# Fused attention and two MoE blocks on one core: q rounded on ScalarE one step sooner, and the first chunk's set-up put in another order

## The chip, the cores and the metric

The kernel runs on 1 core of a Trainium2 chip. The time is device microseconds of one execution of the whole kernel; the figure given for a kernel is the median of its runs, and lower is better.

## The reference

Talking-heads attention over 4 batches of 12 heads (448 positions, head size 64), and behind it two feed-forward blocks over 1792 tokens of width 768, all in float32.

```
scores = scale * q @ k.T                      # per batch and head
scores = einsum('bhij,hg->bgij', scores, w_pre)
attn   = softmax(scores over j)               # eps 1e-9 in the sum
attn   = einsum('bhij,hg->bgij', attn, w_post)
x      = attn @ v
a, b   = x @ w1, x @ w2
x      = ((a * b) @ w3) @ w_out               # first block
h      = relu(x @ w_in)
out    = (h * h) @ w_out2                     # second block
```

## The kernel before

**Rounding in two parts.** TensorE multiplies rounded operands here. So q and k are each split into a rounded "high" part and a "low" rest. For q, `high_q` (L254) writes `qh` from the raw `qraw`, and `low_q` (L262) writes `ql = qraw - qh` on GpSimd. For k, the raw keys are loaded twice, in both halves of the 128 partitions; `high_k` (L231) rounds all of them into `kt`, and `low_k` (L239) replaces the lower half by the rest, in two pieces of 64x448, one for each of the two heads of the tile. `scores` (L271) then needs two matmuls per head, one with `qh` and one with `ql`.

**Chunks, blocks, steps.** The query rows of a batch are cut into 4 chunks (110, 110, 110, 118 rows), 16 chunks in all. A chunk's scores for 12 heads are evacuated to the tile `s` (`evac`, L287). `regroup` (L296) moves them by DMA, SBUF to SBUF, into blocks `r` of up to 120 partitions (10 rows by 12 heads), 11 or 12 blocks per chunk, 180 in all. Per block there is a head mix on TensorE (`premix`, L305, tile `sp`), a row maximum on VectorE (`nm`), the exponential with its sum on ScalarE (`expo`, L317), a split of the probabilities into two f16 parts, and the second mix (`tmix`, L367). `pv` (L416) multiplies by v, twice per chunk. A step of the main loop handles two blocks; step d mixes blocks 2d and 2d+1, and moves blocks 2d+4 and 2d+5.

**What sets the order.** The order is written out by hand, and each engine works its queue strictly in that order. `attention_plan` (L445) puts a chunk's `scores`, and ahead of them `load_q`, `high_q` and `low_q`, on steps; `attention_step` (L492) issues them. In a step SyncE (SP) first issues the regroups, then the loads of q, k and v. `ORDER` (L475) gives each engine's order within a step: VectorE's list ends with `high_q`, `high_k`; `low_q` follows one step behind `high_q`. There are 2 buffers for `qraw`, 2 for `sp`, 6 for `r`.

**The start (L922 to L956).** SP issues q and k loads of chunk 0, then `setup_load` (the tiles `eye`, `w2a`, `w2b`), then the last two k loads, which wait for buffers. Heads 0 to 11 of chunk 0 follow in pairs, with `setup_pre` (it makes the mixing matrix `kpre`) in between. In the first chunk ScalarE does `high_k` and `high_q`, VectorE does both pieces of `low_k`, and evacuations alternate. `setup_post` (the factors of the second mix, with one small matmul `pc`, L207) comes after step -1, that is directly ahead of the first `premix`. `load_v` of batch 0 is issued in step 0. For chunk 1 `load_q` and `high_q` lie in the steps from -5 on, and the scores in the steps from -2 on.

After the attention the two feed-forward blocks run on TensorE, with `mm3` (L53) at its core; nothing of that is changed.

Of the kernel before, what the change touches and what calls it, by code (L numbers as in the profile page):

```python
# [36 lines left out]
def fused_kernel(ctx, tc, q, k, v, w_pre, w_post, w1, w2, w3t, wo, win, wo2, eye, out):  # L37
# [124 lines left out]
    class Attention:  # L162
# [17 lines left out]


        def setup_load(self):
            nc.sync.dma_start(self.eye, eye)
            for t, w in ((self.w2a, w_pre), (self.w2b, w_post)):
                nc.sync.dma_start(t, w)

        def setup_pre(self):
            e, w = self.eye, self.w2a
# [7 lines left out]
        def setup_post(self):  # L196
            kw, kab, ones = (self.kc.tile([120, S], F, tag="p", name=x, bufs=5) for x in ("kw", "kab", "ones"))
            kw, kab = (x[:, :120].rearrange("p (g i) -> p g i", i=10) for x in (kw, kab))
            ones = ones[:, :128]
            nc.vector.memset(ones, 1.0)  # L200
            nc.vector.tensor_tensor(
                kw, self.eye.unsqueeze(1).to_broadcast([120, 12, 10]),
                self.w2b.unsqueeze(2).to_broadcast([120, 12, 10]), ALU.mult,
            )
            nc.vector.tensor_scalar(kab.bitcast(I32), kw.bitcast(I32), 0x7FFFFFFF, None, ALU.bitwise_and)
            pc = self.ps.tile([128, 120], F, tag="sp", name="pc", bufs=2)
            nc.tensor.matmul(pc, ones, kab.rearrange("p g i -> p (g i)"), start=True, stop=True)  # L207
            m, u = self.wm, self.wu
            nc.vector.tensor_reduce(m, pc, AX.X, ALU.max)
            nc.vector.tensor_scalar(m, m, 2.0**-98, None, ALU.max)  # L210
            nc.vector.tensor_scalar(m.bitcast(I32), m.bitcast(I32), 0x7F800000, None, ALU.bitwise_and)
            nc.vector.reciprocal(u, m)
            nc.vector.tensor_scalar(self.iv, m, 2.0**-27, None, ALU.mult)
            nc.vector.memset(self.ivm, 0.0)
            for z in range(2):
                half = slice(64 * z, 64 * z + 64)
                nc.vector.tensor_copy(self.ivm[half, z : z + 1], self.iv[half])
            nc.vector.tensor_scalar(kw, kw, u[:120], 2.0**13, ALU.mult, ALU.mult)
            kh, kl = self.khl
            nc.vector.tensor_copy(kh, kw)  # L220
            nc.vector.tensor_tensor(kl, kw, kh, ALU.subtract)
# [17 lines left out]
        def low_k(self, b, r):  # L239
            raw, t = self.kraw.pop((b, r)), self.kt[b, r]  # L240
            for e in range(2):
                eng = nc.gpsimd if b else nc.vector
                eng.tensor_tensor(t[64:128, e], raw[64:128, e], f32(t[64:128, e]), ALU.subtract)  # L243
            self.done.add(("k", b, r))

# [8 lines left out]
        def high_q(self, n, g4):  # L254
            th = self.ka.tile([128, 4 * IC], R, tag="qh", name=f"qh{n}_{g4}", bufs=3)
            th = self.qh[n, g4] = th[:, : 4 * CHUNKS[n % 4][1]]
            if n:
                nc.vector.tensor_copy(th, self.qraw[n, g4])
            else:
                nc.scalar.activation(th, self.qraw[n, g4], AF.Copy)  # L260

        def low_q(self, n, g4):  # L262
            tl = self.ka.tile([128, 4 * IC], R, tag="ql", name=f"ql{n}_{g4}", bufs=3)
# [181 lines left out]
    def attention_plan():  # L445
# [2 lines left out]
        def add(step, kind, *a):  # L448
            ev.setdefault(step, {}).setdefault(kind, []).append(a)

        lo = {n: (first[n - 1] - 1 - RG) // 2 + 1 for n in range(1, 16)}
        for n in range(16):
            b = n // 4
            if n:
                hi = (first[n] - RG) // 2
                for h in range(NH):
                    t = lo[n] + h * (hi - lo[n]) // NH
                    add(t, "scores", n, h)
                    if h % 4 == 0:
                        add(t - 3, "load_q", n, h // 4)  # L460
                        add(t - 2, "high_q", n, h // 4)
            for y in range(2):
                add((first[n + 1] + 5 + (5 if n < 15 else 0) * y) // 2, "pv", n, y)
        for b in range(1, B):
# [2 lines left out]
                add(t - 1, "load_k", b, r)  # L467
                add(t, "high_k", b, r)
        for b in range(B):
            add((first[4 * b] - 6) // 2 if b else 0, "load_v", b)  # L470
        return ev

    ORDER = (  # L475
        ("premix", "scores", "tmix", "pv"),
        ("expo", "evac", "p_hi", "p2_act", "pv_out"),
        ("rowmax", "p_lo", "norm_recip", "p2_dve", "high_q", "high_k"),
        ("norm_add", "low_q", "low_k"),
    )  # L480
    NEEDS = {
# [433 lines left out]
    with tc.manual_schedule(), ExitStack() as base:  # L915
# [6 lines left out]
        A.load_q(0, 0)  # L922
        A.load_k(0, 0)
        A.load_k(0, 1)
        A.load_q(0, 1, nc.scalar)
        for r in (2, 3):
            A.load_k(0, r)
        A.setup_load()
        for r in (4, 5):
            A.load_k(0, r)  # L930
        for x in range(NH // 2 + 1):
            if x == 0:
                A.split_q(0, 0)
                A.load_q(0, 2)
            if x == 2:
                A.split_q(0, 1)
            if x == 3:
                A.setup_pre()
            if x == 4:
                A.split_q(0, 2)  # L940
            if x < NH // 2:
                A.high_k(0, x)
                A.low_k(0, x)
                for h in (2 * x, 2 * x + 1):
                    A.scores(0, h)
            if x:
                for h in (2 * x - 2, 2 * x - 1):
                    A.evac(0, h)
        step = iter(range(-5, (first[16] + 5) // 2 + 2))
        closed = (first[15] - RG) // 2  # L950
        M = Moe(pre)
        tail = M.tail_plan()
        for d in step:
            attention_step(A, d, ev)
            if d == -1:
                A.setup_post()  # L956
            if d == closed:
                sa.close()
                M.place(pool(sa, "wp"))
# [72 lines left out]
```

## Time and profile before

| | us |
|---|---|
| median of 3 runs | 1325.92 |
| lowest and highest of them | 1325.01, 1327.96 |
| the profiled execution | 1324.3 |
| its span, first to last instruction | 1322.5 |

| engine | busy us | share of the span |
|---|---|---|
| PE (TensorE matmul) | 1284.4 | 97% |
| DVE (VectorE) | 865.6 | 65% |
| ACT (ScalarE) | 696.8 | 53% |
| POOL (GpSimd) | 470.1 | 36% |

The page of the profile gives busy shares of each engine over the span; the views of the trace give single instructions with their start in microseconds from the first instruction, how long the engine was idle before them, and what ended that wait. PE's busy time is modelled from pipelined matmuls, so a matmul whose successor was late can look longer than it worked.

### The profile page before, as it was taken

The numbers are of one execution on the slowest core, as the hardware profiler recorded it, in microseconds if no ns is written. First come the engines' busy times: TensorE is split into PE (matmuls) and PEld (weight loads), VectorE is DVE, ScalarE is ACT, GpSimd is POOL, SyncE is SP. The second block draws the span as 40 slices with busy tenths as digits, with TensorE's granted clock in tenths as the row PEclk, the third lists the DMA queues.
The fourth block names the chain that finished last, engine by engine and source line by source line (L and its number), as shares of the span: only waits on it lengthen the run. The fifth ranks groups of instructions, "written<-read, shape, count | busy, mean of one in ns | idle before, by whom it ended". The sixth has DMA issues, their size and how long they took to land.

```text
span 1322.5 us, 23360 instructions
## 1 busy us (share of the span) xinstructions
PE 1284.4 (97%) x8516; PEld 1111.8 (84%) x8516; DVE 865.6 (65%) x1585; ACT 696.8 (53%) x1542; POOL 470.1 (36%) x522
## 2 busy tenths in 40 slices
PE   5999999999998999999999999999999999999998
PEld 3677776776775788899999999999999999999998
DVE  4899899899879876643127833769565337735742
ACT  4887878787877654443224533534344225534530
POOL 1265255245324512002222322336767322322331
PEclk7999999999999999999999999999999999999999
DMA  5666466566566667655123432463221233433441
GB/s 177 187 178 197 125 197 199 140 173 199 162 159 186 194 196 220 218 164 155 62 81 103 136 116 80 121 220 98 93 62 58 66 92 108 157 94 82 128 147 52
DMA packets 99399, 184.51 MB, mean 140 GB/s; under 512 B 20949, under 2 KB 68053, under 8 KB 98773
## 3 DMA queue, kind: packets, MB, share of 16 engines
q1 hardware_dynamic: 87333, 173.00, 43.9%
q10 hardware_dynamic: 11952, 10.03, 2.3%
q8 instruction: 67, 1.10, 0.3%
q14 instruction: 47, 0.39, 0.1%
HBM read 124.01 MB, written 20.45 MB: 109 GB/s over the span
## 4 chain that ended last, share of the span: by engine, by line
PE 76%; DVE 9%; issue 6%; DMA 3%; POOL 3%; ACT 2%; SPq 0%; POOLq 0%; ACTq 0%; DVEq 0%
PE l L57 39%; PE y L57 9%; PE p L57 5%; PE sp L308 5%; PE tp L373 4%; PE sc L282 3%; DVE pl L364 3%; PE pv L425 3%; DVE nm L314 2%; DMA kraw<-k 1%; DVE p L387 1%; DMA qraw<-q 1%; DMA r<-s 1%; POOL wl L142 1%; POOL ql L265 1%
## 5 line engine op out<-in xcount | busy, mean ns | idle before, releaser
L142 POOL TENSOR_TENSOR wl<-f,wh 128x384 fp32r<-128x384 f32 (+1 forms) x144 | 166.8, 1159 | 468.6 <-ACT wh L114 448.4
L98 DVE TENSOR_SCALAR f<-y 128x384 int32<-128x384 int32 (+1 forms) x176 | 133.4, 758 | 88.2 <-ACT y L86 87.6
L308 PE MATMUL sp<-r,kpre 120*120 120x448 f32 x360 | 158.7, 562 | 10.2 <-ACT p L322 6.8
L322 ACT ACTIVATE p<-sp,nm 120x448 f32<-120x448 f32 x180 | 113.5, 641 | 72.5 <-DVE nm L314 72.2
L364 DVE SCALAR_TENSOR_TENSOR pl<-p,sm,ph 120x448 f16<-120x448 f32 (+3 forms) x270 | 142.0, 579 | 0.3 <-POOL ph L350 0.3
L57 PE MATMUL l<-bhh,wh 128*128 128x448 f32 x384 | 139.3, 363 | 0.0
L57 PE MATMUL l<-blh,wh 128*128 128x448 f32 x384 | 138.8, 362 | 0.0
L57 PE MATMUL l<-bhh,wl 128*128 128x448 f32 x384 | 138.7, 361 | 0.0
L114 ACT ACTIVATE wh<-f 128x384 fp32r<-128x384 f32 (+1 forms) x160 | 89.9, 562 | 74.2 <-DVE f L100 66.7
L100 DVE SCALAR_TENSOR_TENSOR f<-raw,f 128x384 int32<-128x384 int32 (+1 forms) x176 | 124.5, 708 | 6.1
L314 DVE TENSOR_REDUCE nm<-sp 120x1 f32<-120x448 f32 x180 | 106.7, 617 | 24.8 <-PE sp L308 20.9
L373 PEld LDWEIGHTS <-ph 120*128 120x128 f16 x1260 | 93.0, 98 | 30.2 <-issue 22.6
L348 ACT ACTIVATE ph<-p,sm 120x448 f16<-120x448 f32 (+1 forms) x180 | 107.5, 660 | 19.9 <-DVE sm L342 15.7
L282 PE MATMUL sc<-kt,qh 128*110 128x448 f32 (+1 forms) x192 | 100.8, 525 | 11.3 <-DVE kt L243 10.1
L373 PE MATMUL tp<-kwh,ph 120*128 120x120 f16 x630 | 106.0, 217 | 4.2 <-DVE p L389 2.0
L373 PE MATMUL tp<-kwh,pl 120*128 120x120 f16 x630 | 105.0, 216 | 0.0
L373 PE MATMUL tp<-kwl,ph 120*128 120x120 f16 x630 | 105.0, 216 | 0.0
L308 PEld LDWEIGHTS sp<-r,kpre 120*120 120x120 f32 x360 | 59.0, 184 | 53.5 <-issue 22.2
L86 ACT ACTIVATE y<-raw 128x384 f32<-128x384 f32 (+1 forms) x176 | 103.0, 585 | 1.0 <-issue 0.3
L337 POOL TENSOR_SCALAR sm<-sm 120x2 f32<-120x2 f32 (+3 forms) x94 | 25.0, 266 | 212.4 <-ACT p L322 209.1
L293 ACT ACTIVATE s<-sc 110x448 f32<-110x448 f32 (+1 forms) x186 | 90.9, 559 | 7.0 <-PE sc L282 6.9
L887 ACT ACTIVATE r<-l 128x448 f32<-128x448 f32 x64 | 34.9, 545 | 110.1 <-PE l L57 110.1
(620 smaller groups left out, 3272.1 us busy)
## 6 DMA issues: line engine op xcount, KB each, us to landing
r<-s SPq DMA_DIRECT2D x172, 210.0 KB
raw<-win SPq DMA_DIRECT2D x64, 384.0 KB
raw<-wo SPq DMA_DIRECT2D x48, 512.0 KB
raw<-w SPq DMA_DIRECT2D x32, 384.0 KB
kraw<-k SPq DMA_DIRECT2D x24, 448.0 KB
raw<-w3t SPq DMA_DIRECT2D x16, 512.0 KB
qraw<-q SPq DMA_DIRECT2D x35, 220.0 KB
v<-v SPq DMA_DIRECT2D x4, 1536.0 KB
```

The lines of the kernel that those rows point to most:

```text
L57: nc.tensor.matmul(acc, w, x, start=(first and i == 0 and j == 0), stop=(last and i == n - 1 and j == 2), skip_group_check=again,)
L86: nc.scalar.activation(y, self.raw[i][:, :, 1].bitcast(F), AF.Prelu, scale=2.0**-112, alpha=-(2.0**32))
L98: nc.vector.tensor_scalar(fi, yi, 3, None, ALU.logical_shift_left)
L100: nc.vector.scalar_tensor_tensor(fi, raw[:, :, 0], 29, fi, ALU.logical_shift_right, ALU.bitwise_or)
L142: eng.tensor_tensor(self.out[i][1], self.ft.pop(i), f32(self.out[i][0]), ALU.subtract)
L282: nc.tensor.matmul(sc[:ic], t[:, hh * ic : hh * ic + ic], self.kt[b, h // 2][:, h % 2], start=(i == 0), stop=(i == 1))
L308: nc.tensor.matmul(t[:kk], self.kpre[:kk, :kk], self.rt.pop(g)[:kk], start=True, stop=True)
L314: nc.vector.tensor_reduce(nm[:kk], self.sp[g][:kk], AX.X, ALU.max, negate=True)
L322: nc.scalar.activation(p[:kk], self.sp.pop(g)[:kk], AF.Exp, bias=self.nm.pop(g)[:kk], accum_out=self.sm[g // 2][:kk, g % 2 : g % 2 + 1],)
L348: nc.scalar.activation(h[:, to], p[:, fr], AF.Copy, scale=sm)
L364: nc.vector.scalar_tensor_tensor(l[:, to], p[:, fr], sm, h[:, to], ALU.mult, ALU.subtract)
L373: nc.tensor.matmul(t[:, j], p[:, at : at + 128], w, start=(i == 0), stop=(i == 2))
```

## The change

It has two parts. In the **first chunk**: `setup_load` and the second q load are issued from ScalarE's queue, and `setup_post` and `setup_pre` are computed ahead of the first scores; what `setup_post` does last (the split of the second mix's factors) becomes `setup_mix` and comes behind the first chunk. 26 matmuls on a zeroed tile, whose result nobody reads (`warm`), are put ahead of the first scores and between the pairs of heads. Of `low_k`, the second piece goes to GpSimd. The first two q groups of chunk 1 are loaded and split within the first chunk, v of batch 0 is loaded there too, and the scores of chunk 1 begin two steps sooner.

In **all chunks**: `high_q` is done by ScalarE, as the last thing of its step, and for chunks 1 to 15 `load_q`, `high_q` and `low_q` come one step sooner against the scores that need them.

```
         def setup_load(self):
-            nc.sync.dma_start(self.eye, eye)
-            for t, w in ((self.w2a, w_pre), (self.w2b, w_post)):
-                nc.sync.dma_start(t, w)
+            for t, w in ((self.eye, eye), (self.w2b, w_post), (self.w2a, w_pre)):
+                nc.scalar.dma_start(t, w)
+            nc.vector.memset(self.phl[0][0][:, :S], 0.0)
+            self.spare = self.ps.tile([128, S], F, tag="tp", name="spare", bufs=2)
+
+        def warm(self, n):
+            z = self.phl[0][0]
+            for _ in range(n):
+                nc.tensor.matmul(self.spare, z[:, :128], z[:, :S], start=True, stop=True)
...
             nc.vector.reciprocal(u, m)
+            self.kw = kw
+
+        def setup_mix(self):
+            m, u, kw = self.wm, self.wu, self.kw
...
-                eng = nc.gpsimd if b else nc.vector
+                eng = nc.gpsimd if b or e else nc.vector
...
-            if n:
-                nc.vector.tensor_copy(th, self.qraw[n, g4])
-            else:
-                nc.scalar.activation(th, self.qraw[n, g4], AF.Copy)
+            nc.scalar.activation(th, self.qraw[n, g4], AF.Copy)
...
-        lo = {n: (first[n - 1] - 1 - RG) // 2 + 1 for n in range(1, 16)}
+        lo = {n: (first[n - 1] - 1 - RG) // 2 + 1 - 2 * (n == 1) for n in range(1, 16)}
...
-                    if h % 4 == 0:
-                        add(t - 3, "load_q", n, h // 4)
-                        add(t - 2, "high_q", n, h // 4)
+                    if h % 4 == 0 and (n, h) not in ((1, 0), (1, 4)):
+                        add(t - 4, "load_q", n, h // 4)
+                        add(t - 3, "high_q", n, h // 4)
...
-            add((first[4 * b] - 6) // 2 if b else 0, "load_v", b)
+            if b:
+                add((first[4 * b] - 6) // 2, "load_v", b)
...
-        ("expo", "evac", "p_hi", "p2_act", "pv_out"),
-        ("rowmax", "p_lo", "norm_recip", "p2_dve", "high_q", "high_k"),
+        ("expo", "evac", "p_hi", "p2_act", "pv_out", "high_q"),
+        ("rowmax", "p_lo", "norm_recip", "p2_dve", "high_k"),
...
         A.load_k(0, 1)
+        A.setup_load()
         A.load_q(0, 1, nc.scalar)
-        for r in (2, 3):
+        for r in (2, 3, 4, 5):
             A.load_k(0, r)
-        A.setup_load()
-        for r in (4, 5):
-            A.load_k(0, r)
+        A.warm(6)
+        A.setup_post()
+        A.setup_pre()
+        A.warm(8)
         for x in range(NH // 2 + 1):
             if x == 0:
                 A.split_q(0, 0)
                 A.load_q(0, 2)
             if x == 2:
                 A.split_q(0, 1)
-            if x == 3:
-                A.setup_pre()
+                A.load_q(1, 0)
             if x == 4:
                 A.split_q(0, 2)
+                A.load_q(1, 1)
+                A.load_v(0)
             if x < NH // 2:
                 A.high_k(0, x)
                 A.low_k(0, x)
                 for h in (2 * x, 2 * x + 1):
                     A.scores(0, h)
+                A.warm(2)
             if x:
                 for h in (2 * x - 2, 2 * x - 1):
                     A.evac(0, h)
+            if x > 4:
+                A.split_q(1, x - 5)
+        A.setup_mix()
...
-            if d == -1:
-                A.setup_post()
```

## Rows read from the trace of the kernel before

**Rows 1.** The page, busy time, share of the span and instructions by engine

```profile
PE 1284.4 (97%) x8516; PEld 1111.8 (84%) x8516; DVE 865.6 (65%) x1585; ACT 696.8 (53%) x1542; POOL 470.1 (36%) x522
```

**Rows 2.** Stretches: start:end, length, busy and count by engine, PEclk, DMA, GB/s

```profile
61.00:172.00 111.00, 109.89 (x1138) 80.34 (x1135) 100.34 (x228) 89.19 (x220) 47.89 (x74) 1.00 0.58 168
172.00:280.00 108.00, 104.45 (x1062) 76.23 (x1061) 97.32 (x220) 84.67 (x211) 47.63 (x73) 1.00 0.60 176
280.00:396.00 116.00, 113.00 (x1160) 82.52 (x1160) 101.66 (x233) 90.86 (x224) 49.73 (x76) 1.00 0.60 175
...
620.00:900.00 280.00, 280.00 (x1402) 262.45 (x1401) 145.75 (x204) 112.02 (x226) 83.87 (x71) 1.00 0.39 117
```

**Rows 3.** Stretches of the start (columns: PE, PEld, DVE, ACT, POOL)

```profile
15.00:20.00 5.00, 3.50 (x9) 1.71 (x8) 3.87 (x7) 2.80 (x5) 0.81 (x1) 0.70 0.18 45
...
24.00:28.80 4.80, 2.76 (x8) 1.85 (x8) 0.89 (x4) 2.16 (x4) 0.00 (x0) 0.50 0.63 173
...
33.00:37.00 4.00, 4.00 (x13) 2.41 (x12) 2.01 (x5) 4.00 (x11) 1.74 (x3) 0.86 0.95 294
```

**Rows 4.** Timeline of the start: start, duration, instruction, count, idle before and its releaser

```profile
8.90 1.16 DVE L243 TENSOR_TENSOR kt<-kraw,kt 64x448 fp32r<-64x448 f32 x2 [1.50 <-ACT kt L236]
...
9.84 1.22 POOL L265 TENSOR_TENSOR ql<-qraw,qh 128x440 fp32r<-128x440 f32 x1 [4.04 <-ACT qh L260]
...
10.53 5.63 SPq L251 DMA_DIRECT2D qraw<-q  x3
...
10.75 1.33 DVE L243 TENSOR_TENSOR kt<-kraw,kt 64x448 fp32r<-64x448 f32 x2
...
20.12 0.62 DVE L290 COPY s<-sc 110x448 f32<-110x448 f32 x1 [0.79 <-PE sc L282]
...
20.81 1.81 SPq L300 DMA_DIRECT2D r<-s  x2
...
27.25 0.39 DVE L258 CAST qh<-qraw 128x440 fp32r<-128x440 f32 x1 [5.79 <-DMA qraw<-q]
...
28.23 0.78 PE L207 MATMUL pc<-kab,ones 120*128 120x120 f32 x2 [2.04 <-DVE kab L205]
...
28.80 3.19 PE L308 MATMUL sp<-r,kpre 120*120 120x448 f32 x4
28.88 1.65 SPq L412 DMA_DIRECT2D v<-v  x1
...
41.67 1.77 PE L308 MATMUL sp<-r,kpre 120*120 120x448 f32 x4 [1.43 <-DMA r<-s]
...
44.76 1.76 PE L308 MATMUL sp<-r,kpre 120*120 120x448 f32 x4 [0.21 <-ACT p L322]
```

**Rows 5.** The chain that ended last, its pieces with q's transfers: start, duration, what

```profile
10.53 3.47 DMA qraw<-q
...
32.91 10.04 DMA qraw<-q
```

**Rows 6.** Waits from 40 to 600 us: total, times, longest

```profile
ACT p L322 <- DVE nm L314: 67.0, 47, 3.3
...
DVE qh L258 <- DMA qraw<-q: 9.7, 9, 3.4
PEld sc L282 <- POOL ql L265: 9.7, 18, 0.9
...
PE sc L282 <- POOL ql L265: 1.3, 5, 0.3
```

**Rows 7.** Groups by line: busy us, mean ns of one, idle before

```profile
L258 DVE CAST qh<-qraw 128x440 fp32r<-128x440 f32 (+1 forms) x45 | 24.2, 539 | 15.5 <-DMA qraw<-q 15.5
...
L260 ACT ACTIVATE qh<-qraw 128x440 fp32r<-128x440 f32 x3 | 1.7, 568 | 2.4 <-DMA qraw<-q 2.4
...
L243 POOL TENSOR_TENSOR kt<-kraw,kt 64x448 fp32r<-64x448 f32 x36 | 41.9, 1183 | 1.5
```

**Rows 8.** Timeline, ScalarE's exponential of one step with no idle time before it

```profile
180.33 0.66 ACT L322 ACTIVATE p<-sp,nm 120x448 f32<-120x448 f32 x1
```

## The prediction, made before the changed kernel was run

> **What bounds the kernel now.** I read four views, in this order. First the page: TensorE (PE) is busy for 1284.4 of 1322.5 us [rows 1]. Only 38 us of idle can be won by better order alone; work taken off another engine counts only where PE waits for that engine. Second the stretches, to see where these 38 us lie [rows 2]. From 620 to 900 us PE is busy in all 280.00 us: what the attention wins moves the feed-forward blocks forward as they stand, and nothing of it is lost or gained there. Between 61 and 396 us, the steady attention, PE idles 1.11 + 3.55 + 3.00 = 7.7 us, while VectorE (DVE) is busy 100.34 of the first 111.00 us and ScalarE (ACT) 89.19. Nearly everything else lies ahead of 61 us, above all ahead of the first premix. Third the timeline of the start [rows 4]: the last score of chunk 0 is evacuated at 20.74 us (20.12 + 0.62), SP starts the first regroup at 20.81, and the first premix begins only at 28.80. The reader is to see why. Ahead of the premix PE has the small matmul `pc`, which waits for `kab` on DVE; DVE's queue stood 5.79 us at the rounding of a q group whose transfer landed at 27.25. So the premix waited for a q load, not for its own blocks. Fourth, the premix of step 3 at 41.67 waited 1.43 us for a regroup. It was queued behind the load of v, issued at 28.88; in the chain a q load that took 3.47 us at 10.53 took 10.04 us at 32.91, behind the same v [rows 4, 5].
>
> **The start, part by part.** I follow it to one mark, the premix of step 4, at 44.76 now [rows 4].
>
> The last evacuation. Each tile of k has its two pieces of `low_k` on DVE, 1.16 us together. With one piece on GpSimd (POOL), which takes 1.18 us for it [rows 4, 7], the pair ends no earlier than now if both run freely, and 0.62 later if one waits for the other (0.58 + 1.18 against 1.16). The trace shows the second, in part: the pair that started at 10.75 while POOL worked on `ql` took 1.33 instead of 1.16 us, and that `ql` took 1.22 [rows 4]. POOL's work in the first chunk grows to 6 x 1.18 + 5 x 1.22 = 13.2 us, for which it has from about 6 to 20 us: just enough. Behind POOL's `ql` of chunk 1 there waits a q load on SP, and behind that the regroup. DVE gets 6 x 0.58 = 3.5 us off. I take the first regroup at 20.8, as now, between 19.5 (free) and 22.5 (each of the six pairs late by 0.6, in part absorbed).
>
> The Trainium skill (SBUF — State Buffer, section "Who interferes with whom") says that a DVE instruction with two SBUF inputs and a GpSimd instruction that reads SBUF exclude each other, and that the later one waits out the whole of the earlier. That speaks against splitting `low_k` over the two engines. By it the sum below would be smaller by about 1 us; the trace agrees in direction, with 0.17 us on the one pair.
>
> The load of v. It is 1536 KB. It moves to the stretch from 15 to 20 us, where the DMA engines are 18% busy and move 45 GB/s. At the 294 GB/s of the stretch that holds it now it takes 5.4 us [rows 3]: issued behind the third of the q loads that SP issues from 10.53 to 16.16 [rows 4], and with the 2 us or so that a q load needs beyond its bytes (3.47 against 0.8 at this rate), it is done at about 24. What it no longer holds up are the regroups of steps 3 and 4 and the next q load (10.04 - 3.47 = 6.6 us). What it may hold up instead is the first regroup, queued right behind it on SP.
>
> The first premix. `setup_post` and `pc` are gone from that place, and the q group they waited for (the third of chunk 1) is rounded on ACT. Then the premix waits for the landing of its blocks. The trace doesn't give that landing; the q loads nearby took 3.47 us (10.53) and 4.5 us (22.73 + about 4.5 = 27.25) [rows 4, 5]. I take 4.4: first premix at 25.2 instead of 28.80, 3.6 us won; bounds 24 and 28.
>
> Steps 0 to 4. Regroups of 215 KB at 173 GB/s land one per 1.24 us [rows 3]. The eight of steps 0 to 3, with one q load between, need 25.2 + 8 x 1.24 = 35.1; step 3 starts at about 35 instead of 41.67. Step 4 follows one step later. Steps there take 3 to 4 us as DVE and ACT allow, so I take 39 instead of 44.76: **5.8 us** won; bounds 1.5 (regroup late, landing slow) and 9. The two scores of chunk 1 that move ahead of the first premix are in this (four matmuls).
>
> The clock. From 24.00 to 28.80 TensorE has the lower level (0.50 granted, 1.2 GHz) after PE was busy only 3.50 of 5 us from 15 to 20 [rows 3], and the first premix group takes 3.19 us against 1.76 at 44.76, at 1.00 [rows 4]. The 26 extra matmuls fill gaps of PE in chunk 0, where ACT and DVE hand over k; they cost nothing while those are late, at most 0.4 us each where not. What the level is worth is 1.4 us on one step, hidden by the landings at 1.24 us each; I add nothing.
>
> Moves with one answer: the set-up loads leave SP's queue and join ACT's, two more q loads come ahead of v. An issue takes under 1 us (1.81 for two at 20.81 [rows 4]), in stretches where these queues wait anyway; zero.
>
> **The steady steps, part by part.**
>
> q one step sooner. PE's weight loads waited 9.7 us in 18 places for `ql`, PE itself 1.3 us [rows 6]. With `low_q` a full step ahead these waits go. What they cost lies between 1.3 and 9.7; a wait under a running matmul is free, so I take **3.5**. Late next would be the `low_k` of the next batch on POOL.
>
> Off DVE: 45 roundings, 24.2 us [rows 7]. DVE also waited 9.7 us there for q's transfers [rows 6], and behind such a wait stood the row maximum, for which ACT waited in 47 steps. On the path lies only what PE then waited for, of 7.7 us idle in all; bounds 0 and 7.7, and I take **2.5**.
>
> Onto ACT: 45 more at 0.568 us = 25.6 us [rows 7]. They are the last item of a step, so queued behind each is the next step's exponential, and behind that the next premix (2 buffers of `sp`). In 47 of 90 steps ACT waits 1.43 us on average ahead of the exponential (67.0 / 47) [rows 6]: there the rounding is free. In the others the exponential starts with no idle time, as at 180.33 [rows 8], and is late by up to 0.57. Some of these hold a `pv`, whose matmuls cover that. If 25 of 45 fall on a full step and half of these are covered, it is 12 x 0.57 = 6.8 at most; only a part reaches PE, and I take **-3**, between 0 and -25.6. A q transfer that is late now stops ACT instead of DVE; the lead of the load (one step) is unchanged.
>
> Sum: 5.8 + 3.5 + 2.5 - 3 = 8.8 us. The profiled execution took 1324.3, so 1315.5; it lies 1.6 below the median of the runs, 1325.92, so the median after should be **1317**.
>
> **Rivals.**
>
> A, slower: ACT takes DVE's place as the late engine. For: it is full in nearly half of the steps, and the new item is dearer (0.568 against 0.539) and ahead of the exponential, not of a copy that can slip. Against: its 80% in the steady stretches (89.19 of 111.00) become some 87% (25.6 us over the 380 us or so of attention), below DVE's 90% of today. It decides from the point where more than 5.8 + 3.5 + 2.5 = 11.8 us reach PE, that is 21 of 45 roundings uncovered; with 30 it is 17 - 11.8 = +5, so 1331.
>
> B, same: the start's gain is handed back. v, now ahead of the first regroup on SP, and POOL's 13.2 us in the first chunk put the first premix at 28 or later; the steady steps even out. Against: v is 5.4 us in an idle stretch. Time: 1.5 + 3.5 + 2.5 - 6 = 1.5 won, 1324.
>
> C, more: the start at its bound (9), the waits for `ql` at 6 and DVE's relief at 4, ACT for -3: 16 won, 1310.
>
> D, that the change doesn't do what it says: the q load on SP still waits for a `ql` on POOL ahead of the regroups, so the start keeps a wait of another name. It gives what B gives and is counted there.
>
> **How the numbers follow.** Forecast (4 to 13 us won, 1313 to 1322): 0.62. C: 0.14. B: 0.15. A: 0.09. The range that leaves out A and the ends of B and C is 1309 to 1324. About 0.2% (2.7 us) is what a measurement of this kernel can tell from no change: below 1323.3 is faster, 0.62 + 0.14 + 0.01 = 0.77; same is 0.14; slower 0.09.
>
> **What would show it.** Right: the first premix at 24 to 27 us with no wait of `pc` ahead of it; premix of step 4 near 39; no wait of PE's weight loads for `ql` past 40 us; the roundings of q on ACT with hardly any idle time ahead of them. Wrong: a first premix that waits for a regroup past 28 us; PE waiting for ACT's exponential in many more steps; PE idle between 61 and 396 us above 7.7 us; a gain in the attention that is missing from the start of the stretch in which PE is always busy.

## The result and the profile after

The changed kernel takes 1312.72 us (median of 6 runs, 1311.49 to 1316.63), the kernel before beside it 1326.94 (6 runs). The ratio is 0.9899, 95% interval 0.9881 to 0.9917: **faster by 1.0%**, 11 to 16 us. A second set of runs gave 1313.01 against 1324.73, ratio 0.9916 (0.9902 to 0.9929), 9 to 13 us. The forecast was 8.8 us, with a range down to 1309: the sign and the range held, the size was some 3 to 5 us short. The profiled execution took 1316.63 us, 3.9 above its own median, so the second profile is used beside it below; its marks carry the name "again".

The page of the kernel after, busy time by engine, to be read against [rows 1]:

```profile
span 1314.7 us, 23355 instructions
...
PE 1284.7 (98%) x8542; PEld 1112.2 (85%) x8542; DVE 845.5 (64%) x1535; ACT 716.8 (55%) x1587; POOL 472.8 (36%) x528
```

TensorE's busy time is what it was (1284.4 before), with 26 matmuls more. 20 us went from VectorE and 20 came to ScalarE. The span lost 7.8 us, all of it idle time of PE.

Stretches of the kernel after (columns as in [rows 2]):

```profile
58.40:168.00 109.60, 108.28 (x1123) 79.91 (x1124) 92.41 (x212) 94.02 (x230) 47.03 (x75) 1.00 0.59 170
168.00:274.00 106.00, 104.75 (x1076) 77.49 (x1074) 92.08 (x210) 91.34 (x227) 46.95 (x73) 1.00 0.62 182
274.00:388.00 114.00, 111.54 (x1150) 82.10 (x1149) 96.28 (x220) 96.81 (x238) 48.58 (x76) 1.00 0.61 174
620.00:900.00 280.00, 280.00 (x1402) 262.44 (x1401) 150.76 (x207) 111.23 (x223) 86.30 (x71) 1.00 0.39 117
```

In the steady attention PE now idles 1.32 + 1.25 + 2.46 = 5.0 us (7.7 before), with ScalarE as busy as VectorE. The blocks behind are unmoved: PE busy in all 280.00 us, and from the first `y` matmul to the end every kernel of this study took 681.2 us.

The start of the kernel after (timeline, columns as in [rows 4]):

```profile
5.93 1.18 DVE L211 TENSOR_SCALAR kab<-kw 120x120 int32<-120x120 int32 x1
...
10.13 1.16 DVE L253 TENSOR_TENSOR kt<-kraw,kt 64x448 fp32r<-64x448 f32 x2
...
14.10 2.91 POOL L253 TENSOR_TENSOR kt<-kraw,kt 64x448 fp32r<-64x448 f32 x2
...
17.33 1.38 DVE L253 TENSOR_TENSOR kt<-kraw,kt 64x448 fp32r<-64x448 f32 x1 [0.44 <-ACT kt L246]
...
18.62 0.43 SPq L419 DMA_DIRECT2D v<-v  x1
...
22.86 1.84 SPq L307 DMA_DIRECT2D r<-s  x2
...
27.10 1.01 PE L315 MATMUL sp<-r,kpre 120*120 120x448 f32 x2 [1.60 <-DMA r<-s]
...
38.00 1.76 PE L315 MATMUL sp<-r,kpre 120*120 120x448 f32 x4 [0.33 <-ACT p L329]
```

v is issued at 18.62 instead of 28.88, `pc` is gone from the place ahead of the first premix, and that premix waits for its blocks alone. But the first regroup comes 2 us later than in [rows 4], and so the premix starts at 27.10. Step 3 starts at 38.00 without the 1.43 us of waiting for a regroup; it waits 0.33 for ScalarE.

Waits of 58 to 388 us in the kernel after (us in total, times, longest), to be read against [rows 6]:

```profile
ACT p L329 <- DVE nm L321: 40.7, 39, 2.5
...
DVE kt L244 <- DMA kraw<-k: 5.8, 5, 2.3
...
PE sp L315 <- ACT p L329: 3.4, 4, 1.3
```

No wait for `ql` is left, of PE or of its weight loads. In the same stretch of the kernel before ScalarE waited 57.9 us for the row maximum, in 40 places, and PE 4.3 us for ScalarE. So of the signs named in the forecast three are there: no `pc` ahead of the first premix (which starts at 27.10 and 26.18 in the two profiles, at the late edge of the 24 to 27 named), no wait for `ql`, and roundings on ScalarE with hardly any idle time ahead of them (one wait for a q transfer, 1.6 us, in the start). The fourth, step 4 near 39, is missed by 2 to 3 us. A new wait, VectorE's for a k transfer, stands in the second line.

Where the time went, from the start of the premix of each step (step 0, 4, 8; the steps 8 to 79 are the steady part), in the profiles of all kernels that ran:

| kernel | first score | first regroup | step 0 | step 4 | step 8 | steps 8 to 79 |
|---|---|---|---|---|---|---|
| before | 6.92 | 20.81 | 28.80 | 44.76 | 61.01 | 331.19 |
| after | 10.81 | 22.86 | 27.10 | 41.87 | 58.38 | 326.33 |
| after, again (e1) | 9.94 | 21.79 | 26.18 | 40.71 | 57.22 | 325.88 |
| e2 start part only | 9.54 | 21.86 | 26.13 | 39.76 | 56.00 | 332.53 |
| e3 q part only | 6.88 | 21.10 | 25.82 | 47.68 | 63.31 | 324.90 |
| e4 set-up later | 6.51 | 21.91 | 25.87 | 40.02 | 56.52 | 326.44 |
| e5 e4, k on VectorE | 6.90 | 22.62 | 26.83 | 41.52 | 58.02 | 326.35 |
| e6 v late | 9.65 | 21.86 | 26.29 | 46.54 | 63.03 | 326.44 |
| e7 q on ScalarE, no lead | 10.83 | 23.05 | 27.15 | 41.26 | 56.84 | 327.62 |
| e8 lead, q on VectorE | 10.36 | 22.75 | 27.15 | 41.11 | 56.71 | 327.43 |
| e9 set-up last, k on VectorE | 6.72 | 21.30 | 27.95 | 41.12 | 57.62 | 326.00 |
| e10 set-up last | 6.50 | 21.55 | 27.90 | 41.12 | 57.64 | 325.48 |
| e11 no idle matmuls | 10.81 | 23.21 | 27.30 | 41.17 | 57.67 | 327.28 |
| e12 e2, load one step sooner | 9.81 | 21.82 | 26.10 | 39.56 | 55.86 | 331.79 |

### The profile page after: what moved, and what is told of

It reads as the page before. It is cut to its first block, busy times and chain, and to the rows that moved or that the text cites. A ratio compares the mean times of both kernels' runs of the same rounds, so it can differ in the third digit from the quotient of the medians.

```text
span 1314.7 us, 23355 instructions
## 1 busy us (share of the span) xinstructions
PE 1284.7 (98%) x8542; PEld 1112.2 (85%) x8542; DVE 845.5 (64%) x1535; ACT 716.8 (55%) x1587; POOL 472.8 (36%) x528
## 4 chain that ended last, share of the span: by engine, by line
PE 83%; issue 4%; DVE 4%; DMA 3%; ACT 3%; POOL 2%; SPq 0%; ACTq 0%; POOLq 0%; DVEq 0%
PE l L57 39%; PE y L57 9%; PE sp L315 8%; PE tp L380 5%; PE p L57 5%; PE pv L432 5%; PE sc L289 4%; DMA r<-s 1%; DVE pl L371 1%; DMA kraw<-k 1%; POOL wl L142 1%; ACT ph L355 1%; DVE p L394 1%; DVE nm L321 1%; ACT p L329 1%
## 5 line engine op out<-in xcount | busy, mean ns | idle before, releaser
L371 DVE SCALAR_TENSOR_TENSOR pl<-p,sm,ph 120x448 f16<-120x448 f32 (+3 forms) x270 | 137.6, 563 | 0.3 <-POOL ph L357 0.3
```

What stands on the lines that cost most here:

```text
L371: nc.vector.scalar_tensor_tensor(l[:, to], p[:, fr], sm, h[:, to], ALU.mult, ALU.subtract)
```

## The experiments

Edits are against the changed kernel unless they say otherwise.

### The two parts by themselves

e1 is the changed kernel once more. e2 takes the q part back for chunks 2 to 15, and for the last group of chunk 1 the engine alone:

```
-            nc.scalar.activation(th, self.qraw[n, g4], AF.Copy)
+            if n > 1 or (n and g4 > 1):
+                nc.vector.tensor_copy(th, self.qraw[n, g4])
+            else:
+                nc.scalar.activation(th, self.qraw[n, g4], AF.Copy)
...
-                        add(t - 4, "load_q", n, h // 4)
-                        add(t - 3, "high_q", n, h // 4)
+                        x = 1 if n > 1 else 0
+                        add(t - 4 + x, "load_q", n, h // 4)
+                        add(t - 3 + x, "high_q", n, h // 4)
```

and puts `high_q` back into VectorE's list of `ORDER`. e3 is the kernel before with the q part alone; against that kernel:

```
-                        add(t - 3, "load_q", n, h // 4)
-                        add(t - 2, "high_q", n, h // 4)
+                        x = 1 if n > 1 else 0
+                        add(t - 3 - x, "load_q", n, h // 4)
+                        add(t - 2 - x, "high_q", n, h // 4)
```

and `high_q` on ScalarE, as in the changed kernel.

> The changed kernel as it stands, for a second profiled execution. The first one (1316.6 us) lies 3.9 us above the median of its runs, and its trace has TensorE at the lower clock level for 6.8 us at 417 us, in the tail of the attention; the profile of the kernel before has 3.4 us of it at 546 us. If these stretches come and go from execution to execution, this one shows others, and the marks ahead of 400 us stay: first premix 27 us, premix of step 4 at 42, of step 79 at 384 to 385. If they belong to the change, the stretch at 417 us is there again. Time: 0.988 to 0.991 of before either way.

> The changed kernel with q of chunks 2 to 15 as it was before (VectorE, loaded three and rounded two steps ahead); the first chunk's part stays. By the theory that the parts add and that the trace of the changed kernel gives their sizes: premix of step 4 near 42 us instead of 44.8, the steady attention from step 8 to 79 at 331 us as before, so 3 us won, 0.997 to 0.999. By the rival that the first chunk holds most of the gain (5.8 us as predicted, and more behind it): 0.994 to 0.996.

> The kernel before with only the second part: q of chunks 1 to 15 rounded on ScalarE, and of chunks 2 to 15 loaded, rounded and split one step sooner; the first chunk and chunk 1's steps as before. By the theory that the parts add: first premix near 28.8 us as before, steps 8 to 79 in 326 us instead of 331, 0.994 to 0.996. By the rival that the q part only helps where the start has freed the queues: within 0.2% of before.

Measured on one chip: before 1324.73, changed 1313.01, e2 1319.18 (ratio 0.9963, 0.9952 to 0.9975), e3 1321.83 (0.9980, 0.9968 to 0.9992). The start part is worth 5.6 us (3.3 to 6.4 by the interval of the ratio), the q part on top of it 6.2. Alone on the kernel before, the q part brings only 2.9 us, though its steady part is the shortest of all (324.90): it loses at the start. The timeline of e3:

```profile
25.82 2.56 PE L305 MATMUL sp<-r,kpre 120*120 120x448 f32 x4
...
30.74 0.79 SPq L409 DMA_DIRECT2D v<-v  x1
...
42.46 3.32 PE L305 MATMUL sp<-r,kpre 120*120 120x448 f32 x4 [5.63 <-DMA r<-s]
```

Here the first premix starts at 25.82, 3 us sooner than before, with `setup_post` in its old place: the roundings of chunk 1 on ScalarE alone take the q load's wait out of its way. Nothing of it is left at step 4 (47.68 against 44.76): v is still issued in step 0, at 30.74, the steps run into it, and one of them waits 5.63 us for a regroup behind it.

### Which piece carries the start

e6 is the changed kernel with v issued in step 0, as before:

```
         for b in range(B):
-            if b:
-                add((first[4 * b] - 6) // 2, "load_v", b)
+            add((first[4 * b] - 6) // 2 if b else 0, "load_v", b)
...
-                A.load_v(0)
```

> The changed kernel with v of batch 0 loaded in step 0 again. By the theory that v in front of the regroups of steps 3 and 4 is what held those up: first premix 0.5 to 1.5 us sooner than in the changed kernel (25 to 26 us), but the premix of step 4 at 43 to 45 instead of 41 to 42, and 2 to 3 us more in all (0.993 to 0.995). By the rival that v costs the same wherever it stands: step 4 within 0.5 us of the changed kernel, and the same time.

e6 took 1319.28 us (0.9960, 0.9946 to 0.9973). Its timeline:

```profile
30.56 1.53 SPq L419 DMA_DIRECT2D v<-v  x1
...
42.19 3.31 PE L315 MATMUL sp<-r,kpre 120*120 120x448 f32 x4 [6.12 <-DMA r<-s]
...
46.54 1.72 PE L315 MATMUL sp<-r,kpre 120*120 120x448 f32 x4
```

The first premix is where the changed kernel has it (26.29), step 4 is 5 to 6 us later, and the whole kernel some 6 us slower. **Without the early load of v the whole gain of the start is gone.** The other pieces bring the first premix forward, which is worth nothing until v is out of the way. That the early v would be enough without them isn't shown: no run moved it alone.

e4 moves the set-up back behind the third pair of heads, to undo the late first score (10.81 against 6.92). e5 also puts both pieces of `low_k` on VectorE. e9 and e10 move the set-up behind the first chunk, e9 with `low_k` on VectorE, e10 with it split.

e4 and e5:

```
-        A.warm(6)
-        A.setup_post()
-        A.setup_pre()
-        A.warm(8)
+        A.warm(14)
...
+            if x == 3:
+                A.setup_post()
+                A.setup_pre()
```

e9 and e10 have the two calls ahead of `setup_mix` instead. e5 and e9 besides:

```
-                eng = nc.gpsimd if b or e else nc.vector
+                eng = nc.gpsimd if b else nc.vector
```

> The changed kernel with the two set-up computations put behind the second pair of heads instead of ahead of the first scores; the 14 idle matmuls ahead of the first scores stay. In the changed kernel VectorE's first piece of k waits behind the set-up (10.13 us instead of 6.24), the last two loads of k wait for that piece (10.83 instead of 7.47), and the first regroup comes at 22.86 instead of 20.81. By the theory that this is what ate the rest of the predicted gain: first regroup near 20 us, first premix near 24.5, and 2 to 3 us less than the changed kernel (0.986 to 0.989 of before). By the rival that GpSimd's pieces of k set the last evacuation anyway: first regroup after 22 us and a time within 0.1% of the changed kernel.

> As e4, and both pieces of each low k on VectorE again, as in the kernel before. In e4 the first scores start at 6.51 us and the first regroup still comes at 21.91; by the theory that GpSimd's pieces of k (1.45 us each when VectorE works beside them) set the last evacuation, the first regroup now comes at 20 to 20.8 us, the first premix at 24.3 to 25, and the time is 1 to 1.5 us below that of e4. By the rival that the evacuations and ScalarE's rounding set it: regroup at 21.5 to 22 still, no change.

> The changed kernel with the set-up computations behind the whole first chunk (14 idle matmuls stay at the front) and both pieces of each low k on VectorE. In e5 the set-up in the middle held VectorE's fourth low k from about 13 to 15.46 us. By the theory that the first chunk now has nothing but the rounding chain in it: first regroup at 19.5 to 20.5 us (22.86 and 21.79 in the two profiles of the changed kernel), first premix at 24 to 24.8, premix of step 4 at 38.5 to 39.5 (41.87, 40.71), and a time 1.5 to 2.5 us below the changed kernel, 0.988 to 0.990 of before. By the rival that the landings behind v set the first premix: 25.5 to 26.5 whatever the regroup's issue, and no change in time.

> As e9, but with the second piece of each low k on GpSimd as in the changed kernel. By the theory that two pieces side by side on VectorE and GpSimd hold each other up and GpSimd then has the longest queue of the first chunk: first regroup at 21.5 to 22 us, as in e4 (21.91), 1.5 to 2 us later than e9. By the rival that only the set-up's place matters: the same as e9.

Ratios: e4 0.9931 (0.9915 to 0.9947), e5 0.9920 (0.9906 to 0.9934), e9 and e10 both 0.9897 (0.9878 to 0.9916). None differs from the changed kernel by more than the intervals allow. The first score is back at 6.5 to 6.9 us in all four, and the first regroup still comes at 21.3 to 22.6, step 4 at 40.0 to 41.5. That the set-up ahead of the first scores limits the start, which I took for the cause, **is wrong**: something else is late then, as the traces of e5 and e9 show. In e5 it is the set-up block itself, which holds VectorE ahead of a `low_k`:

```profile
12.39 0.17 DVE L206 MEMSET ones<- 120x128 f32 x1
...
16.23 0.42 PE L289 MATMUL sc<-kt,qh 128*110 128x448 f32 x1 [2.57 <-DVE kt L253]
```

In e9 ScalarE waits for the third q load, and later the scores of chunk 1, which stand ahead of the first premix, run at the lower clock (0.57 us each, 0.36 behind them), though the regroup came sooner:

```profile
14.42 0.57 ACT L267 ACTIVATE qh<-qraw 128x440 fp32r<-128x440 f32 x1 [1.50 <-DMA qraw<-q]
...
21.30 7.05 SPq L307 DMA_DIRECT2D r<-s  x6
...
26.50 0.57 PE L289 MATMUL sc<-kt,qh 128*110 128x448 f32 x1
...
27.14 0.36 PE L289 MATMUL sc<-kt,qh 128*110 128x448 f32 x1
...
27.95 0.54 PE L315 MATMUL sp<-r,kpre 120*120 120x448 f32 x1
```

The split of `low_k` makes no difference to the time (e9 against e10), though the two engines plainly stand in each other's way: POOL's two pieces take 2.91 us in the kernel after (timeline above), where one alone took 1.18 in [rows 7], and VectorE's one piece up to 1.38 where two together took 1.16 [rows 4].

e11 takes out the 26 idle matmuls and nothing else (their result was never read).

```
-        A.warm(6)
...
-        A.warm(8)
...
-                A.warm(2)
```

> The changed kernel without the 26 matmuls whose result nobody reads. By the theory that the clock level in the first chunk is hidden by the rounding chain and the landings: TensorE at 1.2 GHz for some 10 to 17 us somewhere between 10 and 34 us, the first premix group at 3 us instead of 2, first regroup and first premix within 0.5 us of the changed kernel, premix of step 4 within 1 us, and a time within 0.1% of it (0.990 to 0.992). By the rival that the clock is what the start gains from: step 4 later by 2 to 3 us and the time 0.993.

e11 took 1316.09 us, 0.9923 (0.9907 to 0.9940). Step 8 comes at 57.67, between the two profiles of the changed kernel: the idle matmuls buy nothing that reaches it. The stretches 6 to 10, 15 to 20 and 27 to 31 us of e11 (columns as in [rows 3]):

```profile
6.00:10.00 4.00, 0.78 (x2) 0.50 (x2) 2.99 (x7) 0.95 (x1) 2.08 (x2) 1.00 0.65 250
...
15.00:20.00 5.00, 4.40 (x11) 2.21 (x10) 3.95 (x6) 3.17 (x6) 4.84 (x5) 1.00 0.35 89
...
27.00:31.00 4.00, 3.23 (x9) 1.55 (x10) 1.25 (x2) 2.42 (x8) 0.95 (x1) 1.00 0.56 151
```

The granted clock is 1.00 in all of them without any idle matmul, where the kernel before had 0.50 from 20 to 31. But 1.00 doesn't mean the faster pace here. Back to back, the score matmuls of e11 start 0.37 us apart up to 23.5 us, as they do at a granted 0.50 in the kernel before (24.1 to 25.2 us), and 0.20 apart behind. In the kernel after, with the idle matmuls, they are 0.20 apart from 11.6 us on. Timeline of e11:

```profile
21.16 0.58 PE L289 MATMUL sc<-kt,ql 128*110 128x448 f32 x1
21.54 0.58 PE L289 MATMUL sc<-kt,qh 128*110 128x448 f32 x1
...
24.03 0.36 PE L289 MATMUL sc<-kt,ql 128*110 128x448 f32 x1
24.23 0.36 PE L289 MATMUL sc<-kt,qh 128*110 128x448 f32 x1
```

So the idle matmuls bring the faster pace some 12 us sooner, and in the kernel after it is lost again: the granted clock is 0.68 from 27 to 31. This falls on step 0. Step 0 in the kernel after, after again, e2 and e11 (columns as in [rows 2]):

```profile
27.10:31.66 4.56, 4.15 (x8) 2.30 (x9) 1.25 (x2) 2.46 (x7) 1.03 (x1) 0.65 0.56 145
```

```profile
26.18:30.50 4.32, 4.15 (x9) 2.29 (x9) 1.25 (x2) 2.29 (x7) 0.87 (x1) 0.62 0.57 148
```

```profile
26.13:29.28 3.15, 2.67 (x8) 1.45 (x9) 1.24 (x2) 0.72 (x2) 0.88 (x1) 1.00 0.57 147
```

```profile
27.30:30.61 3.31, 2.84 (x9) 1.30 (x9) 1.25 (x2) 1.73 (x5) 0.65 (x1) 1.00 0.56 146
```

At 0.65 and 0.62 this step takes 4.56 and 4.32 us, at 1.00 it takes 3.15 and 3.31. Since e11 rounds q on ScalarE as the changed kernel does, it is the clock that makes the step longer and not that engine. Why e2 keeps 1.00 there with the same idle matmuls isn't shown.

Whether e11 is slower than the changed kernel stays open: the two intervals overlap, but on its chip e11 was 3 us above e9 and e10. In its profile 2.4 us lie in the last steps of the attention (steps 79 to 89 take 54.2 us, 51.8 in the second profile of the changed kernel), where PE waits 2.7 us for regroups. The first profile of the changed kernel has such waits too (2.2 us, 53.4 us). In both a drop of the granted clock adds to it: step 81 of e11 takes 9.00 us at 0.81 (6.35 at 1.00 in the second profile of the changed kernel), step 86 of the first profile 9.27 at 0.69 (7.81 at 1.00 in e11). Nothing here ties this to the idle matmuls.

### The two halves of the q part

e7 has q on ScalarE at the old steps, e8 has q on VectorE one step sooner, and e12 is e2 with only the q load one step sooner, with a third buffer for `qraw`:

e7:

```
-                        add(t - 4, "load_q", n, h // 4)
-                        add(t - 3, "high_q", n, h // 4)
+                        x = 1 if n > 1 else 0
+                        add(t - 4 + x, "load_q", n, h // 4)
+                        add(t - 3 + x, "high_q", n, h // 4)
```

e8 has e2's edit of the rounding alone, with `high_q` in VectorE's list. e12 against e2:

```
-                        add(t - 4 + x, "load_q", n, h // 4)
+                        add(t - 4, "load_q", n, h // 4)
...
-            raw = self.ka.tile([128, 4 * IC], F, tag="qraw", name=f"qraw{n}_{g4}", bufs=2)
+            raw = self.ka.tile([128, 4 * IC], F, tag="qraw", name=f"qraw{n}_{g4}", bufs=3)
```

> The changed kernel with q of chunks 2 to 15 rounded on ScalarE, but loaded, rounded and split no sooner than before. Steps 8 to 79 take 326 us in the changed kernel and 332 with q as before. By the theory that the lead is worth 3.5 us and the change of engine about -0.5: 329 to 331 us for these steps, weight loads of the scores waiting some 8 us for the low q again, 3 to 4 us more in all. By the rival that the gain is VectorE's relief: 326 to 327 us, and the time of the changed kernel.

> The changed kernel with q of chunks 2 to 15 on VectorE, but one step sooner as changed. By the theory that the lead is worth 3.5 us: 328 to 329 us for steps 8 to 79 instead of 332, with no waits of PE's weight loads for the low q. By the rival that VectorE's relief is the gain: 331 to 332, and the time of e2 (0.996). With e7 this shows whether the two halves of the q part add to the 6 us.

> As e2 (q of chunks 2 to 15 rounded on VectorE and split where the kernel before did it), but its loads issued one step sooner, with a third buffer for the raw q so that they can be. Steps 8 to 79 took 332.5 us in e2 and 327.4 in e8, where load, rounding and split all come a step sooner on VectorE. By the theory that the lead gains by ending VectorE's waits for q's transfers (4.7 us in 7 places in e2): 328 to 330 us. By the rival that it gains by the place of the rounding and the split among the steps: 332 to 333, and the time of e2, 0.996.

e7 took 1314.45 us (0.9922, 0.9909 to 0.9935), e8 1313.77 (0.9924, 0.9906 to 0.9942), e12 1318.28 (0.9957, 0.9943 to 0.9971). Against the 332.53 us of e2, the steady part is 4.9 us shorter with the engine alone, 5.1 with the lead alone, 6.4 with both: **either half brings most of it, and they don't add**. An earlier transfer alone brings 0.7. Step by step it is plain why. Of the 71 steps 54 take the same time in all seven profiles, to 0.25 us. Steps 18, 41 and 78 go either way; the others are these (us, from the start of the step's premix to the next step's):

| steps | before | e2 | e12 | e7 | e8 | after | again |
|---|---|---|---|---|---|---|---|
| 15, 21, 49, 66, 77 | 26.89 | 26.91 | 26.92 | 26.91 | 24.57 | 24.57 | 24.57 |
| 40 | 5.24 | 5.24 | 5.23 | 3.50 | 3.50 | 3.50 | 3.50 |
| 59 to 61 | 15.41 | 15.94 | 16.84 | 14.76 | 15.38 | 14.77 | 14.86 |
| 19 | 6.65 | 6.65 | 6.63 | 5.99 | 6.13 | 6.12 | 6.13 |
| 32 | 5.56 | 5.63 | 4.76 | 5.21 | 4.38 | 4.75 | 4.57 |
| 35 and 38 | 9.89 | 10.13 | 10.19 | 9.47 | 9.51 | 9.52 | 9.50 |
| 14 | 3.17 | 3.16 | 3.19 | 2.86 | 4.37 | 3.98 | 3.89 |

The first line is the wait for `ql`, and only the lead removes it. Four of PE's five own waits for it [rows 6] lie in these steps and the fifth in step 32; in step 15 it is a weight load that waits, in the kernel before:

```profile
95.69 0.17 PEld L282 LDWEIGHTS sc<-kt,ql 128*110 128x110 f32 x1 [0.69 <-POOL ql L265]
```

Waits of e7, 58 to 388 us, where they are still there:

```profile
PEld sc L289 <- POOL ql L272: 7.9, 14, 0.9
...
PE sc L289 <- POOL ql L272: 1.4, 5, 0.4
```

The removal is worth 26.91 - 24.57 = 2.3 us. The weight loads' waits are free only in part. In the five steps they are 0.69 to 0.85 us long, and the step loses some 0.3 us less than that: 0.37 in step 15, 0.56 in step 77. Of e7's fourteen, seven lie in steps that are longer than in the kernel after by more than 0.25: these five, step 32 by 0.5 (below) and step 60 by 0.4, which step 61 gives back. The seven others cost nothing that can be seen.

The second line is a **collision**. Step 40 of the kernel before, timeline of the engines:

```profile
208.20 2.51 POOL L243 TENSOR_TENSOR kt<-kraw,kt 64x448 fp32r<-64x448 f32 x2
...
209.60 2.38 DVE L364 SCALAR_TENSOR_TENSOR pl<-p,sm,ph 120x448 f16<-120x448 f32 x3
...
211.92 2.25 POOL L243 TENSOR_TENSOR kt<-kraw,kt 64x448 fp32r<-64x448 f32 x2
...
213.28 1.13 DVE L258 CAST qh<-qraw 128x440 fp32r<-128x440 f32 x1
...
214.34 1.14 DVE L314 TENSOR_REDUCE nm<-sp 120x1 f32<-120x448 f32 x2
...
215.82 1.39 PE L308 MATMUL sp<-r,kpre 120*120 120x448 f32 x3 [1.57 <-ACT p L322]
```

and of the kernel after:

```profile
205.18 1.40 DVE L371 SCALAR_TENSOR_TENSOR pl<-p,sm,ph 120x448 f16<-120x448 f32 x3
...
207.72 2.24 POOL L253 TENSOR_TENSOR kt<-kraw,kt 64x448 fp32r<-64x448 f32 x2
...
207.87 1.14 DVE L321 TENSOR_REDUCE nm<-sp 120x1 f32<-120x448 f32 x2
```

While POOL works on `low_k` of the next batch, VectorE's rounding of q takes 1.13 us instead of the usual 0.41; POOL's pair ends at 214.17, the rounding at 214.41. The row maximum stands behind it, behind that the exponential, and behind that the premix, which PE waits 1.57 us for. The rounding isn't alone in this: just ahead, beside the other `low_k`, the three pieces of `pl` (the split of the probabilities) take 2.38 us instead of 1.40. Counted from the step's premix the row maximum starts 2.0 us later than in e7 (3.76 against 1.75), and the rounding is about half of that. In the kernel after the same `low_k` lies beside the row maximum, and neither is any longer for it. The Trainium skill (SBUF — State Buffer, section "Who interferes with whom") says just this: a copy or cast of VectorE in a two-port mode and a GpSimd instruction lock each other out for a whole instruction, a reduction doesn't. The traces agree with both halves: the rounding ends 0.24 us behind POOL's pair, and two row maxima take 1.14 us beside a pair as without one. The durations of all roundings show the same (minimum, median and maximum in ns, first and last start): before, e8 and after.

```profile
L258 DVE CAST qh<-qraw x45: 373/406/1243, 20.8 to 394.0; 128x440 fp32r<-128x440 f32 x33, 128x472 fp32r<-128x472 f32 x12
```

```profile
L268 DVE CAST qh<-qraw x43: 367/389/1214, 26.2 to 379.5; 128x440 fp32r<-128x440 f32 x31, 128x472 fp32r<-128x472 f32 x12
```

```profile
L267 ACT ACTIVATE qh<-qraw x48: 554/600/666, 4.0 to 380.6; 128x440 fp32r<-128x440 f32 x36, 128x472 fp32r<-128x472 f32 x12
```

Seven roundings are over 800 ns in the kernel before, all seven beside a `low_k` on POOL, and none of the other 38 is over 600. e2 and e12 have seven too, e8 has one, ScalarE none. Those before lie in steps 14, 40, 60 and 61, where time is lost, and in 34, 36 and 55, where none is. Step 40 (1.7 us) comes back whether the rounding goes to ScalarE or to another step: the same microseconds, won by either half. No run left the rounding in its place and took GpSimd's work away, so how the 1.7 us divide between the rounding's usual 0.41, what it is held for, and `pl` isn't shown. Of steps 59 to 61 (1.2 us from e2 to after) the engine alone brings all, the lead alone 0.6.

The last line is the price. With the lead, step 14 is 0.8 us longer. Timeline of the kernel after:

```profile
89.48 0.88 DVE L244 CAST kt<-kraw 128x896 fp32r<-128x896 f32 x1 [1.59 <-DMA kraw<-k]
...
91.76 1.76 PE L315 MATMUL sp<-r,kpre 120*120 120x448 f32 x4 [1.11 <-ACT p L329]
```

VectorE now waits there for a k transfer with the row maximum queued behind it; in the kernel before this wait was 2.1 us in 2 places over the whole stretch, now 5.8 in 5. Steps 19, 32, 35 and 38 are 2.0 us shorter together (first profile after, against e2). For step 32 (0.9) e12 shows that the earlier load alone does it; the others were not followed up.

## Why the prediction was right, point by point

**What bounds the kernel.** Held. PE's busy time is the same, the gain is idle time of PE ahead of 400 us, and it reaches the end because the blocks behind are rigid: 681.2 us in every kernel.

**The start, 5.8 us.** The start part alone brings 5.0 us at step 4 (44.76 to 39.76 in e2, where 39 was forecast), and still 5.0 at step 8. In the changed kernel it is 2.9 and 4.1 in the two profiles. Of the steps to it: v's place and the idle stretch that takes it were right (issued at 18.62; 6.6 us were put on the regroups and loads behind it, e6 lost 4.7 to 5.8 at step 4). The lateness of a pair of `low_k` is 0.60 us by its own terms (0.58 + 1.18 against 1.16), not 0.62; nothing hangs on it. The landing was right: 27.10 - 22.86 = 4.2 and 26.18 - 21.79 = 4.4 us from regroup to premix, 4.4 taken. The first regroup "as now" was not: 1.0 and 2.1 us later, the second of them beyond the bound of 22.5. And from the first premix to step 4 it is 41.87 - 27.10 = 14.8 and 14.5 us, against 13.6 in e2 and 13.8 in the forecast. All of this lies in step 0, at the lower clock: 4.56 and 4.32 us against 3.15 in e2, while steps 1 to 3 take 10.21 in both profiles and 10.48 in e2. These two make the difference. What the text didn't see is that the terms are not independent: it counted 3.6 us for the first premix as a gain, and e3 and e6 show that this is lost again at once if v stays. The sum was right because both were in it.

**The idle matmuls and the clock, nothing added.** Right in size for the idle matmuls, as far as e11 and the two profiles can tell. The clock itself is not hidden by the landings, as the text has it: in step 0 of the changed kernel it costs 1.0 to 1.3 us (4.56 and 4.32 against 3.31 in e11).

**q one step sooner, 3.5 us.** It measured 2.3, in five steps. The lower bound, 1.3, was the total of PE's own waits; the cost of a step goes by its weight load's wait, less some 0.3 us. The upper bound, 9.7, was the total of the weight loads' waits, and half of those that e7 has cost nothing. The lead also costs 0.8 us by the k transfer; "late next would be the `low_k` on POOL" named the right stretch and the wrong piece: the transfer ahead of `high_k` is late, not POOL.

**Off VectorE, 2.5 us, and onto ScalarE, -3.** This is the step that failed. Together they were put at -0.5; e7, which is these two alone, is 4.9 us shorter than e2 in the steady part, and gains 10.9 us on the kernel before beside it where e2 gains 5.6. Two terms were mis-sized. The relief was put at 2.5 of the 7.7 us that PE idles, from the total of the 45 roundings. Their average, 539 ns in [rows 7], hides that half of them take 0.41 us or less and seven take 1.0 to 1.2. The wait stands in no list of waits, since VectorE counts as busy. And the price on ScalarE, 12 places with 0.57 us each, of which 3 us were to reach PE, isn't to be found: PE's waits for the exponential are 3.4 us in 4 places against 4.3 in 5. Nor is it seen in the start, where the clock makes step 0 longer.

**The sum.** In the steady part, against e2: 2.3 for `ql`, 2.9 for the steps of the collisions, 2.0 for the four other steps, -0.8 for the k transfer: 6.4 of the 6.2 to 6.6 us measured, where the same terms of the forecast make 3.0. That the whole came out near the forecast is in part luck, since other terms fell short: up to step 8 the kernel after has lost 1.2 to 2.4 us of the 5.0 that e2 wins, and e2's steady part is 1.3 longer than that of the kernel before. By these marks the kernel after is 7.5 to 9.1 us ahead at the end of the steady part (8.8 forecast), the medians are 12 to 14 apart. Rival C had the total about as near from the other side (16 us, 1310), with causes that don't hold: the start was not at 9, nor `ql` at 6.

**Rivals A and B.** A fell: ScalarE is busy in 94.02 of 109.60 us of the first stretch, 86% where 87% was expected, and PE waits for it no more than before. B's mechanism is real in part, since the first regroup is 1 to 2 us late, but not v: its transfer costs nothing in the new place.

**What stays open.** The 3 to 7 us between the marks and the medians. They lie behind the steady part or in the difference of single executions: the profile of before is 2.6 us below its own median, the first profile after 3.9 above, and steps 79 to 89 take 50.4 to 54.2 us in the profiles of the kernels that ran, the two longest with a drop of the granted clock in one step (0.81 in e11, 0.69 in the first profile after). No run was made that settles it.

## What to carry to other kernels

Look at the spread of an instruction's durations, not only at its mean: a cast that takes 0.4 to 0.6 us 38 times and 1.0 to 1.2 us 7 times is waiting inside itself, for another engine, and its neighbours at those seven places say for which; moving it to another engine or to another place then gives the same gain once, not twice. Move a large load out of the way of small ones first: what is won ahead of it is lost at it. Where a wait is to be priced, go by the steps and not by the list: it has 1.3 us of PE's own waits and 9.7 of its weight loads', and 2.3 us came back. Where the clock of TensorE matters, look at how far apart its matmuls start, beside the granted clock.

## What the hardware showed that was not expected

- Work of GpSimd lengthens VectorE's instructions far beyond their own time: the rounding (128x440, f32 to fp32r) took 1.13 us beside `low_k`, 0.38 alone ten microseconds earlier. In the start of the kernel after `kab` (120x120) took 1.18 us beside a `low_k` that started with it, at 5.90 us, and 0.22 in the kernel before, where GpSimd did nothing. The first piece of `pl` took 1.60 us ahead of step 40 of the kernel before, beside `low_k`, and 0.68 in the kernel after.
- Two engines on the two pieces of one `low_k` were no faster than one after the other: GpSimd's pair took 2.91 us instead of 2.25, VectorE's piece 0.80 to 1.38 instead of 0.62, and e9 and e10, without and with the split, took the same time.
- A granted clock of 1.00 did not say that TensorE ran at its faster pace: in the start of e11 it is 1.00 throughout, and the score matmuls start 0.37 us apart up to 23.5 us and 0.20 apart behind.
- A weight load of the scores that waited 0.69 to 0.85 us for `ql` made its step 0.37 to 0.56 us longer, in step 15 without a wait of PE in the list.
